# A delta-rule attention and SwiGLU kernel on one core: the order of work at its begin is rearranged

## The chip, the cores and the metric

The kernel runs on one NeuronCore of a Trainium2 chip. The core has five engines with an instruction queue each: TensorE (PE, matrix products), VectorE (DVE), ScalarE (ACT), GpSimd (POOL) and SyncE (SP, which here only issues DMAs). Each runs its own instructions strictly in the order of the program and waits for the others through semaphores. The metric is the device time of one execution in microseconds (us); times before are given as the median of three runs. A profile is the record of one execution, taken by the hardware profiler.

## The reference

Two blocks, one after the other. The first is a delta-rule attention over B = 4 batches, H = 8 heads, S = 768 steps, head dimension D = 48:

```python
k_n = k / (norm(k) + 1e-06)
for t in range(S):
    y[t]  = q[t] @ state
    v_old = state.T @ k_n[t]
    state = state + beta[t] * outer(k_n[t], v[t] - v_old)
```

The second is a SwiGLU feed-forward network on its output, laid out as 3072 tokens of 384 channels: `(silu(x @ w_gate) * (x @ w_val)) @ w_out`, with w_gate and w_val 384 x 1536 and w_out 1536 x 384. All data is float32.

## The kernel before

**Chunks.** The recurrence is cut into 12 chunks of 64 steps. Within a chunk it becomes matrix products: with K the turned (transposed) keys, K K^T is formed (`gram`, L501), a triangular system with it is inverted, the chunk's corrected values uu follow, and from them the chunk's output y, whose transpose is the input x of the network, and the new state. `turned` (L485) transposes k or q on PE; `gram_steps` (L501) forms K K^T or K Q^T into PSUM, and ACT copies it out (L526 for keys, L521 for queries). p_sb[c], the masked K Q^T, is needed only for y: its upper part is cleared by `under_mask` (L540), on GpSimd for chunk 0.

**Chunks 0 and 1.** They share one substitution on DVE (`first_substitution`, L712 and L718, 15 steps) over blocks of 16 steps. The blocks are put together by a short series: N = L Z (`n_products`, L745), where L are the scaled lower parts of K K^T (`low_copies`, L679) and Z the blocks' inverses (`spread_z`, L735 and L737, puts them into ztp[0]). `n_copies` (L751) takes N out of PSUM, and makes of half of it a copy whose two halves of partitions are exchanged (`n_back`, L755). Then uu comes from four groups of products (L959 for chunk 0 in `first_advance`; L1173 and L1200 for chunk 1 in `advance`): Z r, N times that, N again, N again, with DVE sums (`plus`, L1638) and ACT copies in between. The third group uses n_back. Then y = P uu with P = p_sb (L959 again), its transposes (L1048) and the copies to x (L1049), and the new state (`of_state`, L929; copied by L1054).

**The network.** `gate_val` (L1566) makes 256 columns of the hidden layer for one of the chunks 0 and 1: 12 products of PE in four quarters of three, then silu on ACT (L1575) and the product with the value half on DVE (L1577). From chunk 2 on a faster scheme with fewer products is used (L1411 and L1685). For the first two pieces of chunk 0, `chain` is called behind each quarter and puts one step of chunk 1's series there, with some conversion of weights.

**Weights.** They arrive in 42 pieces. `stage(n, after)` loads piece n on SP (L262); with `after` it first puts a one-element copy on GpSimd (L261) that reads piece `after`, so that piece n is only asked for once that one has landed. Each piece lands in a place that is free just then (`place_of`): tiles of h, of w_out, of ztp[1] ("z1"), and for the last ones the chunk 0 key tile ("zb", a_sb) and p_sb. `power_step` (two ACT instructions, L274 and L280) and `convert` (three DVE instructions, L293, L301, L313) turn a piece into the form that the products read. Converting a piece frees its place and issues the load that waits for it.

**Unread products.** `unread`, `small_unread` and `between` (L638, L648, L643) are products on PE whose results nobody reads.

**Order.** The order of all instructions is written out by hand (`tc.manual_schedule`): on each engine they run in the order in which the Python code emits them.

## Time and profile before

| what | us |
|---|---|
| median of 3 runs (lowest, highest) | 676.53 (675.25, 678.05) |
| the profiled execution | 671.1 |
| its span, first to last instruction | 669.4 |
| PE busy, share of the span | 649.4 (97%) |
| DVE busy | 477.2 (71%) |
| ACT busy | 280.4 (42%) |
| POOL busy | 199.4 (30%) |
| first product of the network (L1566) starts | 43.36 |

Times inside the profile are from the span's start. A line of the timeline has the start, the duration, the engine, the source line, the operation, what it writes and reads with the shape, how many were merged, and in brackets how long the engine was idle before it and what released it. A wait is put down to the event that came last. Matrix products of float32 appear as two records each in most rows; the transposes (L485, L1048) as one. The granted clock was 0.999 of full speed over the whole run.

### The profile page before, as it was taken

Reading aid. Unit: us, or ns where it says so; the run is one execution under the profiler, and the core shown is the slowest. Engines: PE = TensorE matmul, PEld = TensorE weight load, DVE = VectorE, ACT = ScalarE, POOL = GpSimd, SP = SyncE. Lnnn points to the kernel's source line nnn. Section 1 sums busy time; section 2 is a strip of 40 time slices with the busy share of each in tenths; the row PEclk is TensorE's granted clock in tenths of the full one; section 3 lists DMA queues with packets and bytes.
Section 4 is the critical chain, followed back from the end, with each engine's and each line's share of the span. In section 5 each row is a group of like instructions: output and inputs, shape, how many; then the busy total and the mean of one; then the engine's idle time right before and its main releaser. Section 6 shows DMA issues by size and latency. Waiting matters only on the chain.

```text
span 669.4 us, 25015 instructions
## 1 busy us (share of the span) xinstructions
PE 649.4 (97%) x10890; PEld 596.9 (89%) x10890; DVE 477.2 (71%) x992; ACT 280.4 (42%) x625; POOL 199.4 (30%) x310
## 2 busy tenths in 40 slices
PE   8889999999999999999999999989999989999997
PEld 5567887766899999999999999989999989999997
DVE  6779889998868767758667758667758655655562
ACT  4788846224335433434433433532433432433330
POOL 7121031035981032880031880030881000000000
PEclk9999999999999999999999999999999999999999
DMA  9666781005831451473453372434363432232321
GB/s 135 144 177 227 206 225 61 2 13 94 228 68 49 100 117 50 93 144 99 106 127 82 85 158 70 100 86 104 67 138 85 101 84 81 56 89 73 78 74 24
DMA packets 147439, 68.57 MB, mean 102 GB/s; under 512 B 123457, under 2 KB 126561, under 8 KB 147329
## 3 DMA queue, kind: packets, MB, share of 16 engines
q1 hardware_dynamic: 144992, 66.48, 41.5%
q8 instruction: 85, 1.39, 0.9%
q10 hardware_dynamic: 2080, 0.39, 0.4%
q14 instruction: 26, 0.20, 0.1%
q0 software_dynamic: 256, 0.10, 0.1%
HBM read 59.08 MB, written 7.86 MB: 100 GB/s over the span
## 4 chain that ended last, share of the span: by engine, by line
PE 81%; DVE 6%; DMA 4%; ACT 3%; issue 3%; SPq 2%; DVEq 0%; ACTq 0%
PE ffn L1411 38%; PE ffn L1685 20%; PE ffn L1595 4%; PE ffn L1566 4%; PE p_py L501 2%; SPq L172 1%; PE p_px L1173 1%; PE p_px L929 1%; PE p_px L501 1%; PE p_py L1075 1%; PE p_py L1092 1%; PE p_px L1156 1%; DMA h_f<-w_s 1%; DMA last_k<-in_k_dram 1%; DMA kn<-in_k_dram 1%
## 5 line engine op out<-in xcount | busy, mean ns | idle before, releaser
L1411 PE MATMUL ffn<-x_t,w_gv 128*128 128x128 f32 x800 | 108.8, 279 | 0.8 <-DVE p_sb L1635 0.6
L1411 PEld LDWEIGHTS ffn<-x_t,w_gv 128*128 128x128 f32 x800 | 97.4, 192 | 3.8 <-DVE p_sb L1635 1.2
L1445 ACT ACTIVATE sil<-ffn 128x256 f32<-128x256 f32 x100 | 36.5, 383 | 116.2 <-PE ffn L1411 109.6
L1411 PE MATMUL ffn<-x_ffn,w_gv 128*128 128x128 f32 x640 | 84.5, 275 | 0.0
L1685 PE MATMUL ffn<-wo_sb,h_f 128*128 128x192 f32 x480 | 83.9, 328 | 0.0
L1685 PEld LDWEIGHTS ffn<-wo_sb,h_f 128*128 128x128 f32 x480 | 77.9, 190 | 0.6
L1411 PEld LDWEIGHTS ffn<-x_ffn,w_gv 128*128 128x128 f32 x640 | 78.0, 192 | 0.3
L828 POOL TENSOR_TENSOR n_b<-mb,half 128x32 f32<-128x32 f32 x5 | 27.6, 5521 | 168.9 <-DVE mb L555 168.9
L586 POOL TENSOR_TENSOR h_f<-zb,mb 128x31 f32<-128x31 f32 (+15 forms) x124 | 69.0, 556 | 18.2 <-DVE mb L575 8.8
L592 POOL TENSOR_TENSOR zb<-zb,h_f 128x31 f32<-128x31 f32 (+15 forms) x124 | 71.2, 574 | 9.7
L1411 PE MATMUL ffn<-x_t,h_f 128*128 128x128 f32 x472 | 64.8, 280 | 1.3 <-DMA h_f<-w_s 1.0
L1411 PEld LDWEIGHTS ffn<-x_t,h_f 128*128 128x128 f32 x472 | 57.3, 192 | 3.3 <-DVE h_f L1635 0.8
L1446 DVE TENSOR_TENSOR h_f<-sil,ffn 128x256 f32<-128x256 f32 x100 | 39.4, 418 | 23.5 <-ACT sil L1445 23.4
L1107 ACT COPY x_ffn<-p_py 32x256 f32<-32x256 f32 (+3 forms) x108 | 39.4, 365 | 29.6 <-PE p_py L1092 27.9
L1635 DVE TENSOR_TENSOR ffn<-p_sb,ffn 128x512 f32<-128x512 f32 x40 | 27.8, 696 | 27.1 <-PE ffn L1411 26.4
L1638 DVE TENSOR_TENSOR ffn<-ffn,p_sb 128x512 f32<-128x512 f32 x40 | 27.2, 689 | 16.0 <-PE ffn L1411 16.0
L1685 PE MATMUL ffn<-last_k,h_f 128*128 128x192 f32 x200 | 36.0, 327 | 0.0
L1638 DVE TENSOR_TENSOR o_sb<-o_sb,ffn 128x192 f32<-128x192 f32 x50 | 17.5, 350 | 24.4 <-PE ffn L1685 23.8
L1566 PE MATMUL ffn<-x_t,w_gv 128*128 128x256 f32 x144 | 33.4, 384 | 0.0
L1685 PEld LDWEIGHTS ffn<-last_k,h_f 128*128 128x128 f32 x200 | 32.9, 190 | 0.1
L1566 PE MATMUL ffn<-x_ffn,w_gv 128*128 128x256 f32 x144 | 31.9, 380 | 0.0
L1411 PE MATMUL ffn<-x_ffn,h_f 128*128 128x128 f32 x232 | 30.9, 276 | 0.0
(345 smaller groups left out, 1176.3 us busy)
## 6 DMA issues: line engine op xcount, KB each, us to landing
h_f<-w_s SPq DMA_DIRECT2D x81, 256.0 KB, 2.8
more_w<-w_s SPq DMA_DIRECT2D x27, 256.0 KB, 2.6
vin<-in_v_dram SPq DMA_DIRECT2D x48, 96.0 KB, 3.3
out_dram<-o_sb SPq DMA_DIRECT2D x48, 96.0 KB, 2.2
kn<-in_k_dram SPq DMA_DIRECT2D x20, 192.0 KB, 4.4
zt<-in_moe_w_out_dram SPq DMA_DIRECT2D x6, 384.0 KB, 4.9
qpad<-in_q_dram SPq DMA_DIRECT2D x36, 64.0 KB, 3.0
w_s<-h_f SPq DMA_DIRECT2D x7, 256.0 KB, 4.3
```

The lines of the kernel that those rows point to most:

```text
L586: engine.tensor_tensor(out=t_v, in0=zb[:, 0 : j + 1, j : j + 1].to_broadcast([128, j + 1, m]), in1=mb[:, j : j + 1, j + 1 : R].to_broadcas ...
L592: engine.tensor_tensor(out=zb[:, 0 : j + 1, j + 1 : R], in0=zb[:, 0 : j + 1, j + 1 : R], in1=t_v, op=ALU.add,)
L828: nc.gpsimd.tensor_tensor(out=n, in0=mb.rearrange("p j i -> p (j i)")[:, 0 : R * R : R + 1], in1=half, op=ALU.pow,)
L1107: nc.scalar.copy(x_all[at % 128 : at % 128 + rows, at // 128].rearrange("p (bp b i) -> p bp b i", bp=NB, b=2), p[64 * half + lo : 64 * hal ...
L1411: nc.tensor.matmul(p[:, u], w(u), moving, start=start and u == 0, stop=True, skip_group_check=True,)
L1445: nc.scalar.activation(silu_of, p[:, 0:2], ACTF.Silu)
L1446: nc.vector.tensor_tensor(out=h_of(c, PAIRS[r][e % 3], e // 3), in0=silu_of, in1=p[:, 2:4], op=ALU.mult)
L1566: nc.tensor.matmul(ps[name][:, i], w_sb[:, t, (f + i) * 128 : (f + i + 1) * 128], xts[c][:, t], start=(t == 0 and i == 0), stop=(t == KT - 1),
L1595: nc.tensor.matmul(p_o, hs[c, f - f % 2][:, f % 2, bp * 128 : (bp + 1) * 128], wo_sb[:, f], start=(f == 0), stop=(f == FT - 1),)
L1635: nc.vector.tensor_tensor(out=out, in0=a, in1=b, op=ALU.subtract)
L1638: nc.vector.tensor_tensor(out=out, in0=a, in1=b, op=ALU.add)
L1685: nc.tensor.matmul(p[x, part], a(f - f % 2)[:, f % 2], b(f), start=not begun and f == 0, stop=f == FH - 1, skip_group_check=True,)
```

## The change

The changed kernel computes the same. All edits lie in the begin and in the handing over to the network's first pieces. (Line numbers of the changed kernel are lower by up to 14: its product L950 is L959 here, its L1552 is L1566.)

- The unread products: 16 small ones become two large ones, four further places are gone or moved, four stand where two stood before n_products, and the four of `between` are removed from `first_advance`.
- K K^T of chunk 2 is formed right behind its turning, in the pair of banks px, before chunk 3 is turned. `low_copies` of chunks 0 and 1 come ahead on ACT, right behind the copies of q's turning.
- n_back is copied on GpSimd from the copy of N in SBUF (new L744), where DVE (chunk 0) and ACT (chunk 1) copied it from PSUM.
- The masks of chunk 0's p_sb (two L540 on GpSimd) are emitted behind the first step of `first_advance` and behind the stagings of pieces 8 and 9. They stood behind the stagings of pieces 6 and 7, one each. Stagings 8 and up follow that first step, too. So GpSimd's order from there is: one-element copies for pieces 2 to 7, the two copies of n_back, copies for 8 and 9, the two masks, copies for 10 to 13, two `spread_z` of chunk 1, copies for 14 to 17, and later the two copies of chunk 1's n_back.
- `spread_z` of chunk 1 moves from DVE and ACT to GpSimd (L726).
- The state of chunk 0 (`of_state` and its copy) is made behind the first quarter of the first gate_val.
- `chain` runs over the first three gate_vals (12 quarters, in 8 of which a step of chunk 0 or 1 stands), with fewer pieces converted in each.
- The last pieces land in ztp[0] ("z0", two places), p_sb and z1; the key tile a_sb is used no more for that.

```diff
@@ -230,13 +230,13 @@
         places[n] = words(hp[n])
     place_of = [(n, 0) for n in range(10)] + [("wo", 8 * H_), ("z1", 0)]
     in_wo, in_z1 = [("wo", 2 * H_ * n) for n in range(4)], [("z1", 2 * H_), ("z1", 0)]
-    in_work = [("zb", 0), ("p_sb", 0)]
+    in_z0 = [("z0", 0), ("z0", 2 * H_)]
     place_of += [("wo", H_ * n) for n in range(8)]
     place_of += [("z1", H_ * n) for n in (2, 3, 1, 0)]
-    place_of += in_wo + in_work + (in_z1 + in_work) * 3
+    place_of += in_wo + in_z0 + (in_z1 + [("p_sb", 0)] + in_z0) * 2 + in_z1
 
     beta_s = places["wo"].bitcast(FP32)[:, 6 * H_ : 6 * H_ + S]
-    LATE = {"zb": 18, "p_sb": 12}
+    LATE = {"z0": 18, "p_sb": 12}
     freed_by = {}
     for n, (name, lo) in enumerate(place_of):
         m = 2 * pieces[n][4]
@@ -612,7 +612,6 @@
             l_sb[c] = a[:, R * R * c : R * R * (c + 1)].rearrange(
                 "p (h k) -> p h k", k=C
             )
-        places["zb"] = words(a)[:, 0 : 2 * PIECE]
         first_of["flat"] = new_mb().rearrange("p k i -> p (k i)")
         first_of["diag"] = first_of["flat"].rearrange("p (j h) -> p h j", j=R)
         first_of["zb"] = places["z1"].bitcast(FP32)[:, 4 * H_ - 1056 : 4 * H_]
@@ -636,16 +635,6 @@
 
         for _ in range(count):
             nc.tensor.matmul(p[0:R], half, half[:, 0:1].to_broadcast([128, 512]))
-
-    def between(columns):
-        p = banks("p_t", 0)[0]
-        of = half[:, 0:1].to_broadcast([128, columns])
-        nc.tensor.matmul(p[0:R, 0:columns], half, of)
-
-    def small_unread(count, p):
-
-        for _ in range(count):
-            nc.tensor.matmul(p[0:C, 0:C], ident[0:C, 0:C], ident[0:C, 0:C])
 
     def first_gram(c, tag):
 
@@ -752,7 +741,9 @@
                 n_sb[c][:, par].rearrange("p bp j i -> p (bp j i)"), p_n[par]
             )
         for x in range(2):
-            back(n_back[c][half_of(x)], p_n[1][half_of(1 - x)])
+            back(n_back[c][half_of(x)], n_sb[c][half_of(1 - x), 1].rearrange(
+                "p bp j i -> p (bp j i)"
+            ))
 
     n_back = {}
 
@@ -948,10 +939,10 @@
     def first_advance():
 
         zt = ztp[0][:, 0].rearrange("p (par bp j) i -> p par bp j i", par=2, bp=NB)
-        r, pq = vin.pop(0), p_sb.pop(0)
+        r = vin.pop(0)
         p_n = banks("p_n", 2)
         n_products(0, p_n)
-        n_copies(0, p_n, (nc.scalar.copy, nc.vector.tensor_copy), nc.vector.tensor_copy)
+        n_copies(0, p_n, (nc.scalar.copy, nc.vector.tensor_copy), nc.gpsimd.tensor_copy)
 
         def product(p, at, flip, weights, moving):
             for j in range(NJ):
@@ -992,7 +983,6 @@
                 lambda par, b, j: v[there(par, b), 1 - par, bp, j],
             )
             nc.scalar.copy(uu[:, :, bp], pairs[bp])
-        between(128)
         yield MORE
         for bp in range(NB):
             product(
@@ -1007,7 +997,6 @@
             plus(t[:, 0:2, bp], v[:, :, bp], pairs[bp])
             for x in range(2):
                 nc.scalar.copy(t[half_of(x), 2, bp], t[half_of(1 - x), 0, bp])
-        between(128)
         yield MORE
         for bp in range(NB):
             product(
@@ -1018,10 +1007,9 @@
                 lambda par, b, j: t[there(par, b), 1 - par, bp, j],
             )
             plus(uu[:, :, bp], t[:, 1:3, bp], pairs[bp])
-        between(256)
-        spread_z(1, 0, nc.vector)
         held_loads[26] = lambda: load_v(2)
         yield
+        pq = p_sb.pop(0)
         y = work.tile([128, NB, NJ, 2, D], FP32, name="y", tag="r", bufs=2)
         for bp, copy in enumerate((nc.scalar.copy, nc.vector.tensor_copy)):
             product(
@@ -1047,10 +1035,8 @@
                 at = slice(k * 128, (k + 1) * 128)
                 nc.tensor.transpose(p_f[bp][:, k], y_f[:, bp, at], ident)
             copy(x_v[:, :, bp], p_f[bp])
-            if bp == 0:
-                between(256)
+        yield
         p_s = of_state(0, uu)
-        spread_z(1, 1, nc.scalar)
         nc.scalar.copy(state, p_s)
         yield
 
@@ -1948,29 +1934,27 @@
         first_diag(1, p_g[1])
         spread_beta(copy_a)
         turned(0, True, 0)
+        low_copies(0, p_g[0])
+        low_copies(1, p_g[1])
         nc.vector.transpose(first_of["mb"][:, 0 : R * R], first_of["flat"])
         r_b = first_n()
         first_scale(r_b)
         for n in range(6):
             stage(n, n - 2 if n > 1 else None)
         load_v(1)
-        small_unread(16, banks("p_t", "py")[0])
+        unread(2, banks("p_t", "py")[0])
         turned(2, False, "py")
         first_q = [gram_steps(0, True, 0, (copy_a, copy_a))]
         next(first_q[0])
-        low_copies(0, p_g[0])
-        unread(1, banks("p_t", "py")[0])
+        gram(2, False, "px", (copy_a, copy_a))
         turned(3, False, "py")
-        unread(1, banks("p_t", "px")[0])
+        unread(1, banks("p_t", 2)[0])
         turned(1, True, "px")
-        gram(2, False, "py", (copy_a, copy_a))
-        unread(1, banks("p_t", "px")[0])
-        low_copies(1, p_g[1])
         gram(3, False, "py", (copy_a, copy_a))
         first_q.append(gram_steps(1, True, "px", (copy_a, copy_a)))
         next(first_q[1])
         next(first_q[0])
-        unread(2, banks("p_t", 2)[0])
+        unread(4, banks("p_t", 2)[0])
         first_substitution()
         first_z()
         some, others = slice(0, 1), slice(1, NB)
@@ -1981,20 +1965,22 @@
         scale_v(0)
         next(first_q[1])
         stage(6, 4)
-        next(first_q[0])
         stage(7, 5)
-        next(first_q[0])
-        for n in range(8, 10):
-            stage(n, n - 2)
-        for n in range(10, 18):
-            stage(n, n - 3)
-        for n in range(18, 23):
-            stage(n)
         zb_1 = work.tile([128, R, R], FP32, name="zb", bufs=1)
         new_nt(0, spare_of_q, state_flat[:, LEAD : LEAD + 512])
         new_nt(1, zb_1.rearrange("p k i -> p (k i)"), spare_of_q[:, 0:512])
         gens["advance", (0,)] = [first_advance(), 0]
         step("advance", advance, 0)
+        for n in (8, 9):
+            stage(n, n - 2)
+        next(first_q[0])
+        next(first_q[0])
+        for n in range(10, 14):
+            stage(n, n - 3)
+        for x in range(2):
+            spread_z(1, x, nc.gpsimd)
+        for n in range(14, 23):
+            stage(n, n - 3 if n < 18 else None)
         power_step(0)
         step("advance", advance, 0)
         converts_first(0)
@@ -2006,7 +1992,6 @@
         step("advance", advance, 0)
         power_step(1)
         step("advance", advance, 0)
-        step("advance", advance, 0)
         converts_first(4)
         for n in (3, 5):
             power_step(n)
@@ -2015,25 +2000,31 @@
         power_step(6)
 
         went = []
+        chain_at = (0, 1, 3, 4, 6, 7, 9, 10)
 
         def chain(_):
 
-            if not went:
-                p_n = banks("p_n", 2)
-                n_products(1, p_n)
-                n_copies(1, p_n, (copy_a, copy_a), copy_a)
-            step("advance", advance, 1)
-            n, ahead = ((1, 7), (2, 6), (4, 4))[len(went)] if len(went) < 3 else (2, 4)
-            went.append(n)
-            if len(went) in (4, 5):
-                next(first_q[1])
-            convert(todo[:n], ahead)
-            del todo[:n]
+            at = len(went)
+            went.append(1)
+            n, ahead = (1, 2, 4, 1, 2, 1, 2, 1, 2, 1, 2, 1)[at], (7, 6, 4, 4)[min(at, 3)]
+            if n:
+                convert(todo[:n], ahead)
+                del todo[:n]
+            if at in chain_at:
+                if at in chain_at[4:6]:
+                    next(first_q[1])
+                if at == 0:
+                    step("advance", advance, 0)
+                    p_n = banks("p_n", 2)
+                    n_products(1, p_n)
+                    n_copies(1, p_n, (copy_a, copy_a), nc.gpsimd.tensor_copy)
+                else:
+                    step("advance", advance, 1)
 
         pairs = [(c, f) for c in range(2) for f in range(0, 8, 2)]
         pairs += [(c, f) for f in range(8, FT, 2) for c in range(2)]
         for at, (c, f) in enumerate(pairs):
-            early = c == 0 and f < 4
+            early = c == 0 and f < 6
             if c == 1 and f == 0:
                 finish(1)
                 second_inverse.append(invert(1))
```

## Prediction

> **What bounds the kernel now.** I read the page first, then the span cut into stretches of 5 us, then the timelines of PE, GpSimd and SP in the begin.
>
> ```profile
> PE 649.4 (97%) x10890; PEld 596.9 (89%) x10890; DVE 477.2 (71%) x992; ACT 280.4 (42%) x625; POOL 199.4 (30%) x310
> ...
> PE 81%; DVE 6%; DMA 4%; ACT 3%; issue 3%; SPq 2%; DVEq 0%; ACTq 0%
> ```
>
> PE is busy for 97% of the span and is 81% of the chain that ended last. So what the begin costs is the time until PE has network products to do, and what it waits for afterwards.
>
> ```profile
> 25.00:30.00 5.00, 3.60 (x107) 1.92 (x102) 4.01 (x9) 4.21 (x10) 0.56 (x3) 1.00 0.43 128
> 30.00:35.00 5.00, 4.33 (x232) 3.67 (x224) 3.33 (x6) 3.54 (x9) 1.60 (x3) 1.00 0.49 132
> 35.00:40.00 5.00, 3.40 (x132) 2.51 (x135) 3.98 (x9) 2.58 (x9) 1.42 (x2) 1.00 0.66 167
> ...
> 65.00:70.00 5.00, 5.00 (x26) 4.43 (x25) 5.00 (x17) 3.93 (x11) 0.00 (x0) 1.00 0.73 223
> ...
> 110.00:115.00 5.00, 3.39 (x21) 2.76 (x20) 4.58 (x11) 4.21 (x10) 0.00 (x0) 1.00 0.00 0
> ```
>
> The columns are the stretch, its length, busy us of PE, PE's weight loads, DVE, ACT and POOL, then clock, DMA share and GB/s. From 65 us PE is full, but DVE is, too; it converts weights. At 110 PE loses 1.61 us.
>
> ```profile
> 1.03 4.90 PE L638 MATMUL p_px<-half 128*32 128x512 f32 x6 [1.03 <-DVE half L322]
> ...
> 27.92 1.91 PE L638 MATMUL ffn<-half 128*32 128x512 f32 x4
> 29.76 1.16 PE L745 MATMUL ffn<-zt,a_sb 64*64 64x64 f32 x64
> ...
> 38.84 0.68 PE L959 MATMUL p_px<-uu,p_sb 64*64 64x48 f32 x32 [0.73 <-DVE uu L1638]
> ...
> 42.28 1.15 PE L929 MATMUL p_px<-uu,kn 64*64 64x48 f32 x64
> 43.36 1.56 PE L1566 MATMUL ffn<-x_t,w_gv 128*128 128x256 f32 x6
> ```
>
> Chunk 0's series runs from n_products at 29.76 over the product with p_sb at 38.84 to the first network product at 43.36. GpSimd in that time:
>
> ```profile
> 32.63 0.18 POOL L261 COPY h_f<-h_f 128x1 uint32<-128x1 uint32 x1 [0.45 <-DMA h_f<-in_moe_w_gate_dram]
> 32.77 1.28 POOL L540 TENSOR_TENSOR p_sb<-p_sb,mask_q 128x512 f32<-128x512 f32 x1
> 35.75 0.19 POOL L261 COPY h_f<-h_f 128x1 uint32<-128x1 uint32 x1 [1.70 <-DMA h_f<-in_moe_w_val_dram]
> 35.89 1.28 POOL L540 TENSOR_TENSOR p_sb<-p_sb,mask_q 128x512 f32<-128x512 f32 x1
> 40.27 0.18 POOL L261 COPY h_f<-h_f 128x1 uint32<-128x1 uint32 x1 [3.11 <-DMA h_f<-in_moe_w_gate_dram]
> 40.90 0.18 POOL L261 COPY h_f<-h_f 128x1 uint32<-128x1 uint32 x1 [0.45 <-DMA h_f<-in_moe_w_val_dram]
> ```
>
> These one-element copies are those for pieces 6, 7, 8 and 9; each waits until pieces 4, 5, 6 and 7 have landed. The two masks stand between them, at 32.77 and 35.89, ahead of the waits that end at 40.27 and 40.90. The loads behind those late waits are on SP:
>
> ```profile
> 32.59 3.25 SPq L185 DMA_DIRECT2D vin<-in_v_dram  x4
> 35.94 0.57 SPq L262 DMA_DIRECT2D h_f<-in_moe_w_gate_dram  x1
> 36.60 0.38 SPq L262 DMA_DIRECT2D h_f<-in_moe_w_val_dram  x1
> ```
>
> Piece 6 can't be asked for before 35.94: SP first issues four loads of v, and those stand behind piece 5, which was released at 32.00. Nothing in the change moves this part of SP's or GpSimd's queue.
>
> **Part 1: fewer unread products, K K^T of chunk 2 ahead, low copies ahead.** Removed are 16 small products (2.07 us, 13.55), three of 1.05 us (17.81, 19.81, 23.10), two before n_products (1.91) and four short ones (0.41, 0.41, 0.62, 0.62): 9.2 us. Added are seven large ones at 0.92 to 1.05: 6.7 us. ACT sits idle for 2.39 us before 16.68; the twelve low copies (two rows of 1.68 us) now start at 14.29 and end at 17.65, so the copies of chunk 2's turned keys start 1.0 us later and K K^T of chunk 2 on PE at about 18.3. Following each copy and product from there by the rows, the last K Q^T ends near 24.7 and the four unread products end near 28.3. Z is ready at 28.31 as before, because DVE's substitution is untouched. So n_products starts at 28.4 rather than 29.76: a gain of 1.35 us. It disappears in part 2. Two pauses of PE with no releaser (1.40 at 26.03, 0.74 at 34.80) may move or vanish; they have cover there, too.
>
> **Part 2: n_back on GpSimd.** The two copies come behind the one-element copy for piece 7, which ends at 35.94; N itself is in SBUF at about 30.3. GpSimd has no row for 64x512 copies. The nearest are a memset of 128x256 (0.31, so 0.6 for twice the length) and the two-operand mask (1.28). I take 0.75, nearer the memset since a copy reads one operand; ends: 0.5 and 1.28 each. N_back is ready at 37.4 (36.9 to 38.5). The third group of chunk 0 (34.01 before) waits for it. From 34.01 to the last sum of uu at 39.16 were 5.15 us, 0.74 of them a pause; so uu is there at 41.8 (41.3 to 43).
>
> **Part 3: the masks.** They stand behind the copies for pieces 8 and 9, which end at 41.08, and take 2 x 1.28: ready at 43.64. That is later than uu for either price of part 2, so it decides. Both masks are needed by the second product of the group that starts at 38.84 now; it starts at 43.69, **4.85 us later**. Then its two groups (0.68 and 0.66, without the 0.34 pause of before), DVE's copies of y (0.36 and 0.72), the transposes (0.55) and the copy to x (0.56), with 0.05 between: 47.4 for the first network product, against 43.36. That is **+4.05**. DVE's third conversion (piece 4, done at 44.06 now) follows the copy to x and is done at 48.5, just when the third product wants it: +0.1, cover gone.
>
> **Part 4: the state behind the first quarter.** Its 1.09 us of PE lay ahead of 43.36 and now lie behind: **+1.09**. The ACT copy of it comes behind seven pieces' conversions (0.67 each) and is done at 52.1; the product that needs it (L1156 now) comes at 52.7. No wait.
>
> **Part 5: spread_z of chunk 1 on GpSimd.** DVE loses 0.65 and ACT 1.19. GpSimd does it behind the copy for piece 13, near 47.2, at 0.5 (memset) to 1.9 (the mask, half as much again for the turned read) each; at 1.28 it ends at 49.8, and n_products of chunk 1 wants it at 50.1. At the upper end PE would wait 1 us there. Pieces 14 and up are asked for about 1.5 us later, under a shift of 4.
>
> **Part 6: chunk 1's series over three gate_vals.** Now PE waits 0.56 at 52.49 (for an ACT copy) and 0.72 at 61.23 (for DVE). With two quarters between some steps I find both copies ready: **-1.28**, with 0 as the other end. Pieces 12 to 17 are converted by 68.4, before the third gate_val's value half needs the last, at 71.9.
>
> **Part 7: last pieces in Z's tile.** The 1.61 at 113.56 is PE waiting for ACT's copy of K K^T of chunk 4, which stands behind piece 41's power step, which waits until 109.67 for its load, which waits for DVE. Silu products of DVE run 4 to 5 us behind PE there (104.00 for a piece that PE ended near 99.3). DVE's conversions begin 4.5 us later than before (piece 4) and DVE has few waits to give back, so I keep the 1.61: **0**, ends -1.6 and +0.5. The free key tile does not help: the copy is queued behind piece 41 all the same.
>
> **Sum:** 4.05 + 0.1 + 1.09 - 1.28 + 0 = **+4.0 us**. The profiled execution would go from 671.1 (span 669.4) to 675.1. The median is 5.4 above the profiled one; I carry the difference over: 676.5 + 4.0 = 680.5.
>
> **Rivals.** *PE goes cold.* In the new begin PE has nothing from about 32.0 until n_back at 37.4, then little until 43.7. The rows show PE at two speeds with the granted clock at 1.00 in both: three unread products took 4.90 us at the start, two took 1.91 at 27.92, so 1.63 against 0.96 each. The longest idle stretch of before behind the start is 1.6 us, so its trace doesn't show that a pause brings the slow speed back. If it does, the p_sb groups cost 1.3 more, the transposes on the path 0.5, and a stretch like the 4.9 us of the start does 2.45 us less of work: +4.2, against which the 1.61 is given back: 676.5 + 4.0 + 4.2 - 1.6 = 683.1. [...]
>
> *The shift is taken up later (no change).* If PE's lateness lets DVE and ACT catch up, the 1.61 goes: 4.0 - 1.6 = 2.4, so 678.9. For it: DVE has waits of 1.87 and 1.02 between 80 and 95. Against it: these are behind ACT, which shifts with PE.
>
> *The masks come in time (faster).* If pieces 6 and 7 landed by 36.1 instead of 40.9, the masks would be done by 38.8 and parts 1, 4, 6 and 7 would be left: -1.35 + 1.09 - 1.28 - 1.61 = -3.15, 673.4. Against it are the SP rows: piece 6 is only asked for at 35.94, and the two masks alone take 2.56.
>
> **Chances.** Forecast 0.42, cold 0.30, taken up 0.16, faster 0.12. The range from 676.0 to 685.0 reaches from part 6 and 7's better ends nearly together to the cold case with spread_z's wait. What a measurement of this kernel can tell from no change is 0.5%, 3.4 us: the forecast with its own spread of 1.5 us is slower by that in two thirds of its cases, the cold case nearly always. So faster 0.12, same 0.28, slower 0.60.
>
> **What would show it.** In the profile after: GpSimd's masks back to back at about 41.1 and ending at 43.6, behind one-element copies released by DMA; n_back's copies at 36; PE idle before the third and fifth group; the first network product at 47.4. Cold shows as L1566's rows of three products at over 2 us instead of 1.56. Part 6 shows as no waits over 0.3 between 50 and 75, part 7 as a pause of about 1.6 near 117. The prediction is wrong if the pieces land earlier, or if PE's wait at 113 is gone.

## The result and the profile after

The changed kernel takes **671.98 us** (median of 9 runs, 668.29 to 673.54); the kernel before takes 675.25 us (9 runs in the same set, 670.27 to 678.05). The ratio is 0.9936, with a 95% interval of 0.9907 to 0.9965: faster by 0.64%, where the prediction had 680.5 and slower. The profiled execution of the changed kernel took 672.2 us with a span of 670.5. That is its median, while the profiled execution of before (671.1) lay 4.2 us under the median of this set. Profile against profile the kernel became 1.1 us *slower*, median against median 3.3 us faster; both have to be explained.

The page of the kernel after: the busy time of TensorE (PE), the granted clock in 40 slices of the span, and the shares of the chain that ended last.

```profile
PE 651.4 (97%) x10854; PEld 598.6 (89%) x10854; DVE 476.7 (71%) x989; ACT 279.1 (42%) x622; POOL 208.0 (31%) x316
...
PEclk9968999999999999999999999999999999999999
...
PE 83%; DVE 6%; DMA 4%; SPq 3%; ACT 2%; issue 2%; POOL 0%; DVEq 0%; ACTq 0%; POOLq 0%
```

PE has 36 matmul records fewer (18 unread products), and "issue", the time with no releaser in the profile, is 2% of the chain instead of 3%. In the third and fourth slice (34 to 67 us) the clock digit falls to 6 and 8. GpSimd in the begin (the timeline of the kernel after: start, duration, engine, line, instruction, and in brackets the idle time before it):

```profile
36.65 0.18 POOL L261 COPY h_f<-h_f 128x1 uint32<-128x1 uint32 x1 [0.50 <-DMA h_f<-in_moe_w_val_dram]
36.90 1.26 POOL L744 COPY state<-qpad 64x512 f32<-64x512 f32 x2
...
40.76 0.33 POOL L261 COPY h_f<-h_f 128x1 uint32<-128x1 uint32 x1 [0.34 <-DMA h_f<-in_moe_w_val_dram]
41.05 2.67 POOL L540 TENSOR_TENSOR p_sb<-p_sb,mask_q 128x512 f32<-128x512 f32 x2
...
47.06 4.09 POOL L726 TENSOR_SCALAR zt<-mb,m_rows 128x512 f32<-128x512 f32 x2
```

The copies of N stand behind piece 7's one-element copy, and the masks behind that of piece 9; they end at 43.7. The two spread_z take 2.05 us each. PE in the same stretch:

```profile
27.96 1.16 PE L734 MATMUL ffn<-zt,a_sb 64*64 64x64 f32 x64
...
38.21 0.34 PE L950 MATMUL p_px<-uu,state 64*64 64x48 f32 x1 [4.44 <-POOL state L744]
...
44.61 0.68 PE L950 MATMUL p_px<-uu,p_sb 64*64 64x48 f32 x32 [2.61 <-DVE uu L1624]
...
46.37 1.76 PE L1036 MATMUL ffn<-ident,y 128*128 128x128 f32 x6 [0.36 <-ACT y L1024]
48.88 3.41 PE L1552 MATMUL ffn<-x_t,w_gv 128*128 128x256 f32 x6 [0.74 <-ACT w_gv L274]
```

N_back comes 4.4 us too late for the third group, the masked product starts at 44.61, and the first network product at 48.88 instead of 43.36. Its first three products (six records) take 3.41 us instead of 1.56. The stretches of the kernel after (the columns are those of the prediction's second fence; the clock is the third from the end) show why:

```profile
30.00:35.00 5.00, 2.10 (x89) 1.60 (x81) 1.14 (x3) 3.11 (x8) 0.37 (x2) 1.00 0.48 141
35.00:40.00 5.00, 1.79 (x62) 1.79 (x62) 0.56 (x1) 0.00 (x0) 1.59 (x4) 0.51 0.80 206
...
45.00:50.00 5.00, 3.90 (x61) 2.83 (x53) 2.86 (x6) 4.40 (x14) 3.15 (x4) 0.53 0.66 213
50.00:55.00 5.00, 4.86 (x109) 3.48 (x111) 4.83 (x13) 3.20 (x9) 2.48 (x5) 0.50 0.41 121
...
110.00:115.00 5.00, 5.00 (x143) 4.29 (x141) 4.86 (x12) 3.36 (x7) 0.00 (x0) 1.00 0.65 203
```

PE ran at half clock from 35.1 to 41.9 and from 45.3 to 55.6 us. At 110 to 115 us it is full: the 1.61 us wait of before has gone. So the begin became slower, about as forecast, and yet the kernel is faster. The rest of the document is about where the time came back.

### The profile page after: what moved, and what is told of

Its sections match the earlier page's. It is cut to its first block, busy times and chain, and to the rows that moved or that the text cites. A ratio compares the mean times of both kernels' runs of the same rounds, so it can differ in the third digit from the quotient of the medians.

```text
span 670.5 us, 24923 instructions
## 1 busy us (share of the span) xinstructions
PE 651.4 (97%) x10854; PEld 598.6 (89%) x10854; DVE 476.7 (71%) x989; ACT 279.1 (42%) x622; POOL 208.0 (31%) x316
## 3 DMA queue, kind: packets, MB, share of 16 engines
q8 instruction: 85, 1.39, 0.9%
## 4 chain that ended last, share of the span: by engine, by line
PE 83%; DVE 6%; DMA 4%; SPq 3%; ACT 2%; issue 2%; POOL 0%; DVEq 0%; ACTq 0%; POOLq 0%
PE ffn L1397 39%; PE ffn L1671 20%; PE ffn L1581 4%; PE ffn L1552 4%; DMA h_f<-in_moe_w_val_dram 2%; PE p_px L1159 2%; PE p_px L920 2%; SPq L139 1%; PE p_py L1061 1%; PE p_px L1142 1%; PE p_py L501 1%; PE p_py L1078 1%; PE p_px L501 1%; SPq L185 1%; PE p_py L902 1%
## 5 line engine op out<-in xcount | busy, mean ns | idle before, releaser
L1397 PEld LDWEIGHTS ffn<-x_t,w_gv 128*128 128x128 f32 x800 | 97.4, 192 | 3.6 <-DVE p_sb L1621 1.3
L819 POOL TENSOR_TENSOR n_b<-mb,half 128x32 f32<-128x32 f32 x5 | 30.4, 6073 | 161.1 <-DVE mb L555 161.1
L586 POOL TENSOR_TENSOR h_f<-zb,mb 128x31 f32<-128x31 f32 (+15 forms) x124 | 70.7, 570 | 19.2 <-DVE mb L575 9.7
L1552 PE MATMUL ffn<-x_t,w_gv 128*128 128x256 f32 x144 | 35.4, 397 | 0.9 <-ACT w_gv L274 0.7
L1552 PEld LDWEIGHTS ffn<-x_t,w_gv 128*128 128x128 f32 x144 | 27.2, 195 | 5.7 <-ACT w_gv L274 1.1
L1552 PE MATMUL ffn<-x_ffn,w_gv 128*128 128x256 f32 x144 | 31.9, 380 | 0.0
```

The lines of the kernel that those rows point to most:

```text
L586: engine.tensor_tensor(out=t_v, in0=zb[:, 0 : j + 1, j : j + 1].to_broadcast([128, j + 1, m]), in1=mb[:, j : j + 1, j + 1 : R].to_broadcas ...
L819: nc.gpsimd.tensor_tensor(out=n, in0=mb.rearrange("p j i -> p (j i)")[:, 0 : R * R : R + 1], in1=half, op=ALU.pow,)
L1397: nc.tensor.matmul(p[:, u], w(u), moving, start=start and u == 0, stop=True, skip_group_check=True,)
L1552: nc.tensor.matmul(ps[name][:, i], w_sb[:, t, (f + i) * 128 : (f + i + 1) * 128], xts[c][:, t], start=(t == 0 and i == 0), stop=(t == KT - 1),
```

## The experiments

Each row has the median of all executions of that kernel and its ratio to the kernel before, run in turn on the same chip. The ratio compares runs taken in turn, so it is not the quotient of two medians. The rows come from sets on several chips; the median of before was 675.99 beside the first four rows, 676.28 beside the next four and 678.35 beside the three after them.

| run | edit | us | ratio (95% interval) |
|---|---|---|---|
| before_again | none | 677.19 | 1.0023 (0.9990 to 1.0057) |
| masks_first | after; masks and N's copies ahead of pieces 6 to 9 | 670.43 | 0.9928 (0.9904 to 0.9952) |
| masks_late | before; masks behind pieces 8, 9 | 683.90 | 1.0124 (1.0090 to 1.0158) |
| fewer_unread | before; 18 unread products fewer | 673.04 | 0.9961 (0.9932 to 0.9991) |
| after_padded | after; 18 unread products more | 676.66 | 1.0004 (0.9975 to 1.0033) |
| spread_back | after; spread_z of chunk 1 on DVE | 670.97 | 0.9933 (0.9905 to 0.9960) |
| masks_and_spread | masks_first and spread_back | 668.07 | 0.9874 (0.9833 to 0.9915) |
| masks_spread_warm | masks_and_spread; five unread products more | 668.13 | 0.9877 (0.9831 to 0.9922) |
| before_shifted | before; 16 unread products fewer, same PE time | 672.44 | 0.9941 (0.9906 to 0.9976) |
| before_wide | before; four unread products made wider | 674.95 | 0.9980 (0.9946 to 1.0013) |
| masks_spread_wide | masks_spread_warm, stream as in after | 668.52 | 0.9884 (0.9842 to 0.9926) |
| before_third | none, one profile | 677.83 | one execution |

**The begin, undone and done alone.** masks_late moves the masks in the kernel before and nothing else:

```diff
         stage(6, 4)
-        next(first_q[0])
         stage(7, 5)
-        next(first_q[0])
         for n in range(8, 10):
             stage(n, n - 2)
+        next(first_q[0])
+        next(first_q[0])
```

> The kernel before with only the two masks moved behind the copies for pieces 8 and 9, as the change has them. Theory that the late masks cost what the prediction gave them: the product with p_sb starts near 43.7 instead of 38.84, and the kernel is slower by 4 to 5 us than before, by 6 to 8 with a stretch at half clock. Rival (taken up later): within 2 us of before.

It was slower by 1.2%, about 8 us. PE's longest waits in masks_late (us in total, times, longest):

```profile
PE p_px L959 <- POOL p_sb L540: 5.2, 2, 4.4
PE ffn L1411 <- issue: 3.0, 3, 1.9
PE p_py L911 <- issue: 2.5, 1, 2.5
PE p_px L485 <- ACT a_sb L529: 2.3, 1, 2.3
```

The wait on the masks is the forecast's 4.85 to within half a microsecond. The other three lines are already in the profile of before, at 1.8, 2.0 and 1.6 us; here their totals are larger, and half-clock windows stand at 43.3 to 50.1, behind the stall at L485 (121.8 to 125.2) and behind L911's pause (555.3 to 558.7). So part 3's mechanism costs what was forecast, or more.

masks_first goes the other way, in the kernel after:

```diff
-        stage(6, 4)
-        stage(7, 5)
...
-        for n in (8, 9):
-            stage(n, n - 2)
         next(first_q[0])
         next(first_q[0])
+        for n in (6, 7, 8, 9):
+            stage(n, n - 2)
```

> The changed kernel with n_back's copies and both masks put ahead of the copies for pieces 6 to 9 on GpSimd (behind that for piece 5). Theory that GpSimd's queue delays the begin by 5 us and cools PE: n_back is copied at about 33 instead of 36.9, the masks end near 37 instead of 43.7, the first network product comes at 42 to 43.5 instead of 48.9, and the clock falls to half in no stretch or in one window of 3.4 us; 6 us below the changed kernel, so 664 to 667. Rival (the begin's lateness is taken up later by the conversions of DVE and ACT): the first network product is early, and the end moves by less than 2 us: 670 to 672.

The first network product came at 42.0 instead of 48.9, but the gain was gone 10 us later: 670.43 lies in the range of the expected rival, not of the theory. The clock wasn't kept either; there were four windows of half clock in three stretches (32.2 to 35.6, 42.4 to 45.8, 49.3 to 56.1) where one at most was expected. PE's longest wait in masks_first, and GpSimd's timeline at that place:

```profile
PE ffn L734 <- POOL zt L726: 5.5, 1, 5.5
```

```profile
46.93 0.29 POOL L261 COPY wo_sb<-wo_sb 128x1 uint32<-128x1 uint32 x1 [2.37 <-DMA wo_sb<-in_moe_w_gate_dram]
47.20 4.41 POOL L726 TENSOR_SCALAR zt<-mb,m_rows 128x512 f32<-128x512 f32 x2
```

Chunk 1's spread_z on GpSimd stands behind piece 13's copy, at 47.2 whatever PE does, and takes 4.4 us. In the kernel after, PE is so late that it doesn't notice; with an early begin it is the next wait. Two runs separate this. spread_back puts both on DVE in the kernel after, masks_and_spread does the same in masks_first:

```diff
             plus(uu[:, :, bp], t[:, 1:3, bp], pairs[bp])
+        spread_z(1, 0, nc.vector)
...
             copy(x_v[:, :, bp], p_f[bp])
+        spread_z(1, 1, nc.vector)
         yield
...
-        for x in range(2):
-            spread_z(1, x, nc.gpsimd)
```

> The kernel after with chunk 1's two spread_z on VectorE (0.65 us each in the kernel before), one behind the last sum of chunk 0's series, one behind the last copy of x, instead of GpSimd (2.05 us each). Theory (in the kernel after no TensorE wait hangs on them, since the third group of products is late anyway): 671 to 673, within 0.5% of the kernel after. Rival (GpSimd's two spreads hold up the copies that issue pieces 14 to 17 behind them, and so the conversions): 1 to 2 us faster, 669 to 671.

> The kernel with the masks ahead of the copies for pieces 6 to 9 (masks_first), and chunk 1's two spread_z on VectorE as in spread_back. Theory (the whole shift of the begin was GpSimd's order: masks at 4 to 5 us, then the spreads that took the 5.5 us back): first network product at 42 us as in masks_first, no wait of TensorE on zt at 52 us, every later mark about 5 us earlier than in the kernel after (151 to 153 instead of 158.2 for chunk 1's first product with the state), time 664 to 667. Rival (a clock or conversion bound takes it back: half clock or waits on the weights between 45 and 75 us): the marks within 2 us of the kernel after and a time of 669 to 672.

spread_back can't be told from the kernel after (670.97 against 671.98, ratios 0.9933 and 0.9936); its time lies at the edge between the two expected ranges. masks_and_spread, at 668.07, is 1.26% under before and the fastest here together with its two variants. PE's timeline in masks_and_spread:

```profile
34.63 0.25 PE L950 MATMUL p_px<-uu,state 64*64 64x48 f32 x1 [0.48 <-POOL state L744]
...
38.84 1.11 PE L950 MATMUL p_px<-uu,p_sb 64*64 64x48 f32 x32
...
43.68 2.90 PE L1554 MATMUL ffn<-x_t,w_gv 128*128 128x256 f32 x6 [0.74 <-DVE x_t L1038]
48.25 1.43 PE L734 MATMUL ffn<-zt,a_sb 64*64 64x64 f32 x64
```

The masked product waits for nothing, and chunk 1's n_products start 5.7 us earlier than in the kernel after (53.96 there). Chunk 2's first product of q with the state (L1144 in before) comes at 152.4, within the 151 to 153 expected; the expectations call it chunk 1's first product with the state, and from here on it is called chunk 2's mark. The time was 1 us above the 664 to 667 expected.

**Where the late gain comes from.** The kernel before has two PE pauses without a releaser that no part of the prediction counted: 1.8 us at 444 (L1411) and 2.0 us at 543 (L911). In the kernel after there is none over 0.3 us behind 60 us. PE's timeline in before at the two places, and then that of the kernel after at the second:

```profile
441.65 0.61 PE L1411 MATMUL ffn<-x_ffn,more_w 128*128 128x128 f32 x4
444.08 0.60 PE L1411 MATMUL ffn<-x_ffn,more_w 128*128 128x128 f32 x4 [1.82 <-issue]
...
539.79 1.22 PE L911 MATMUL p_py<-t,z 32*32 32x32 f32 x120
543.00 0.26 PE L911 MATMUL p_py<-t,z 32*32 32x32 f32 x8 [1.99 <-issue]
```

```profile
543.04 1.29 PE L902 MATMUL p_py<-t,z 32*32 32x32 f32 x128
```

One theory: they belong to a place in PE's instruction stream, and 18 products fewer ahead of them moved that place onto other work. The rival: they depend on when data or work arrives. The first run is the kernel before unchanged, the second takes away its unread products alone:

> The kernel before, unchanged, profiled a second time. Theory P (pauses): PE's pauses that no engine releases (1.82 at 444 us and 1.99 at 543 us in the profile before, none in the profile after) belong to the place in PE's instruction stream, so they return here at the same instructions, and the typical execution is longer than the first profile's 671.1 us by more of them. Theory B (begin): the first profile caught a lucky begin, with the granted clock at 0.999; a typical one has a stretch at half clock in the first 60 us, a mean clock of 0.98 to 0.99, and is then near 675. Theory N: both kernels are equal, and the ratio of 0.9936 is chance; then this run's median comes out within 0.3% of the other runs of before, which it must in any case.

```diff
-        between(128)
...
-        between(128)
...
-        between(256)
...
-            if bp == 0:
-                between(256)
...
-        small_unread(16, banks("p_t", "py")[0])
+        unread(2, banks("p_t", "py")[0])
```

> The kernel before with two large unread products for the 16 small ones and without the four of between: 18 products fewer, as in the changed kernel, and nothing else of the change. Theory P: every later instruction of PE stands where it stands in the changed kernel, so the pauses at 444 and 543 us vanish or shrink and the kernel gains 2 to 4 us. Theory B: the begin is as before or cools (fewer products that keep PE busy), and the kernel is equal or slower by up to 3 us.

In before_again the pauses came back at the same two instructions (1.7 and 1.4 us). fewer_unread lost about 6 us in the begin (half clock from 36.9 to 47.1; chunk 2's mark at 157.2 instead of 151.3), had neither pause, and was still 0.4% faster than before. Both theories allow that, since its begin had moved. after_padded settles it: the kernel after, with as many products more as it has fewer, in a place where PE waits anyway.

```diff
-        unread(4, banks("p_t", 2)[0])
+        small_unread(22, banks("p_t", 2)[0])
```

> The kernel after with 22 products of 32x32 where it has 4 unread ones of 128x32 ahead of n_products of chunk 0: 18 more products, so that from there on TensorE's instructions stand at the same places of its stream as in the kernel before. Place theory (the pauses of 1.8 us at 444 us and 2.0 us at 543 us in the kernel before, which have no releaser, hang on where a run of short products falls in TensorE's stream): pauses of 1.4 to 2 us come back near 450 us (L1411) and 549 us (L911 of before, L902 or so of after), and the time rises by 3 to 4 us over the kernel after, to 675 to 676. Rival (these pauses hang on the data transfers or on when the work arrives, which the other parts of the change moved): no pause over 0.7 us after 260 us and a time within 1 us of the kernel after, 671 to 673.

It took 676.66, and the whole gain was gone (ratio 1.0004). PE's timeline in after_padded has only two waits over 0.3 us between 410 us and the end:

```profile
448.63 0.49 PE L1402 MATMUL ffn<-x_ffn,more_w 128*128 128x128 f32 x3 [1.49 <-issue]
...
548.14 0.26 PE L907 MATMUL p_py<-t,z 32*32 32x32 f32 x7 [2.37 <-issue]
```

(L1402 and L907 here are L1411 and L911 in before.) They stand behind 7731 and 9383 matmul records, in before behind 7730 and 9382, with every other part of the change in place. So the place theory holds. The other profiles bear it out: all six with 10890 matmul records have both pauses (1.4 to 2.5 us) at these places, though PE gets to the first one anywhere between 444 and 455 us, and of the eight with fewer records only masks_spread_warm has a pause of over 0.4 us at either. before_shifted is the counterpart: the kernel before, with the begin's PE time kept and its stream 32 records shorter.

```diff
-        between(128)
+        between(384)
...
-        between(128)
+        between(384)
...
-        between(256)
...
-            if bp == 0:
-                between(256)
...
-        small_unread(16, banks("p_t", "py")[0])
+        unread(2, banks("p_t", "py")[0])
```

> The kernel before with 16 unread products fewer at about the same time on TensorE: two of 512 columns (2.1 us) for the 16 of 32x32 (2.1 us), and the four between the groups of chunk 0's series (768 columns in all) as two of 384. All that follows stands 32 matmul records earlier in TensorE's stream. Place theory: the profile's pauses without a releaser at 444 us (1.8 us) and 543 us (2.0 us) shrink to 1 us or less in all while the begin keeps its marks (chunk 1's first product with the state at 151 to 153 us), so 2.5 to 3.5 us faster than the kernel before at equal clock, a median of 672 to 674. Rival (the pauses hang on something else that fewer_unread moved by its 6 us of delay): both pauses stay, 675 to 677.

Both pauses were gone, and its ratio of 0.9941 (a median of 672.44) is as much of a gain as the whole change brought. Its profiled execution is not a clean one: a stall of 2.9 us at L485 and a wait of 2.2 us for a load at 352 us, each with 3.4 us of half clock behind it; chunk 2's mark was at 153.7, a little outside the 151 to 153 expected. The verdict rests on the median and on the missing pauses.

**Why the typical execution of before is slower than its profile.** Two profiles of before (671.1 and 671.7 us) had a granted clock of 1.00 from 5 us to PE's last product, but among 61 executions of it in the first two sets of experiments (the two longest left out), the 23 with a mean clock of 0.9955 or more have a median of 673.75, the other 38 one of 677.16. By estimate (3.41 x 0.5 / 670) a window of 3.41 us at half clock takes 0.0025 off the mean clock of a run of 670 us, so this parts executions with one such window at most from those with two or more. Two runs looked for the place.

```diff
-        between(128)
+        between(512)
...
-        between(256)
+        between(512)
```

> The kernel before with its four unread products between the groups of chunk 0's series 512 columns wide each instead of 128, 128, 256 and 256: no instruction more or fewer, 1.3 us more of TensorE's time, in gaps where it waits 0.3 to 0.7 us. Clock theory (most executions of the kernel before lose 3 to 4 us to one or two windows of half clock in the begin, its profiled executions did not): the mean granted clock is 0.997 or more in most executions, and the median 673 to 674.5, the pauses at 444 and 543 us staying. Rival (the slower executions of before have another cause, or the wider products only delay the groups): clocks of 0.992 to 0.995 as before and a median of 676 to 677.5.

before_wide is inconclusive: 9 of its 12 executions had a mean clock of 0.995 or more, against 6 of the 22 of before beside it, but only 5 had the 0.997 that was expected of most, its interval reaches 1.0013, and its profiled execution was itself one of the long ones (677.39). It did show two windows of half clock: one in the begin, from 28.8 to 32.2, and one from 117.6 to 121.0, behind 2.9 us of stall at L485. So one more profile of before was taken:

> The kernel before, unchanged, one more profile. Where the typical execution of before loses the 3 to 4 us that its two profiled ones did not lose: stall theory (ScalarE's copies of chunk pair 1's first gram products stand behind the conversion of pieces of the output weights that come late, so TensorE stands at L485 near 114 us for over 2.2 us, and a window of half clock follows, as in the profiles of before_wide, before_shifted and masks_late): if this execution is over 674 us, that stall is 2.3 to 3 us with 3.41 us of half clock behind it. Begin theory (the loss lies in half-clock windows ahead of 60 us): half clock there instead, and the stall at 114 us is 1.6 to 2.3 us without one. If the execution is under 673 us, neither is told apart, and the clock is 1.00 until the end.

This execution took 677.83 us, close to the median. PE's waits, and two stretches with a clock under 1:

```profile
PE p_py L911 <- issue: 2.5, 1, 2.5
PE p_py L959 <- issue: 2.4, 3, 1.0
PE ffn L1411 <- issue: 2.1, 2, 1.6
PE p_px L485 <- ACT a_sb L529: 2.0, 1, 2.0
```

```profile
115.00:120.00 5.00, 5.00 (x20) 4.40 (x21) 4.20 (x15) 1.61 (x3) 0.00 (x0) 0.66 0.01 2
```

```profile
545.00:550.00 5.00, 2.47 (x82) 2.31 (x69) 0.83 (x2) 1.02 (x2) 0.00 (x0) 0.87 0.20 74
550.00:555.00 5.00, 5.00 (x37) 5.00 (x37) 2.39 (x4) 1.89 (x4) 0.00 (x0) 0.78 0.29 67
```

Half clock stands at 115.3 to 118.7, behind the stall at L485, and at 548.7 to 552.2, behind L911's pause; none stands ahead of 60 us. For this execution the begin theory is out; before_wide's window at 28.8 leaves it open for others. The stall theory is right on the place, though at 1.95 us this stall is shorter than the 2.3 to 3 expected (before_again had one of 2.28 and no half clock, so its length alone doesn't decide), and it named only half of the loss: the second window hangs on the late pause.

**The clock in the begin.** masks_spread_warm adds five unread products between the groups (the expectation counts six, and five for before, which has four). masks_spread_wide takes two wide ones instead, leaves out one at two earlier places, and has the stream of the kernel after.

```diff
             nc.scalar.copy(v[:, :, bp], pairs[bp])
+        between(256)
         yield MORE
...
             nc.scalar.copy(uu[:, :, bp], pairs[bp])
+        between(128)
         yield MORE
...
+        between(128)
...
+        between(256)
...
+            if bp == 0:
+                between(256)
```

```diff
-        between(256)
...
-        between(128)
+        between(512)
...
-        between(128)
+        between(512)
...
-        between(256)
...
-            if bp == 0:
-                between(256)
...
-        unread(2, banks("p_t", "py")[0])
+        unread(1, banks("p_t", "py")[0])
...
-        unread(4, banks("p_t", 2)[0])
+        unread(3, banks("p_t", 2)[0])
```

> masks_and_spread with six unread products (three of 256 columns, two of 128, and one more of 256 behind the first group) between the groups of chunk 0's series, where the kernel before has five. Theory (the half clock comes from TensorE's gaps between the groups, and filling them keeps it at 1.0): no half-clock window between 30 and 60 us and 1 to 3 us faster than masks_and_spread. Rival (the gaps are too long for six short products, or the half clock lies under waits anyway): within 1 us of masks_and_spread, half clock still there.

> masks_spread_warm with two unread products of 512 columns instead of its five between the groups, and one fewer at two earlier places, so that TensorE's stream stands as in the kernel after (masks_spread_warm has five products more, and a pause of 1.3 us at 542 us). Place theory: no pause over 0.5 us near 542 us, and 666.5 to 667.5. Rival (the pause is a matter of chance, or the half clock of the begin comes back): 668 to 669.

masks_and_spread had half clock from 35.3 to 48.9, masks_spread_warm only from 44.0 to 47.4, yet the first network product came at 43.7 and 44.0, chunk 2's mark at 152.4 in both, and the times are equal (668.07 and 668.13). So the longer half clock cost nothing by that mark; what covered it is not shown. masks_spread_wide had no pause near 542, as the place theory expected (masks_spread_warm had 1.3 us there), but its 668.52 lies in the rival's range, and the gain could not be told from nothing. Its profile has what masks_spread_warm's lacks: a stall of 2.46 us at L485, and two windows of half clock ahead of 60 us (32.6 to 36.1 and 42.9 to 46.3).

## Why the prediction was wrong

The table gives the start of the same work in five profiles, counted in matmul records back from the last one (the first row is the first network product).

| place | before | before_third | after | after_padded | masks_and_spread |
|---|---|---|---|---|---|
| first network product | 43.4 | 43.9 | 48.9 | 47.9 | 43.7 |
| 8526 from the end (chunk 2's mark) | 151.3 | 154.4 | 158.2 | 156.0 | 152.4 |
| 7100 | 227.4 | 231.6 | 233.6 | 231.3 | 227.9 |
| 3165 (ahead of L1411's pause) | 441.5 | 446.2 | 446.9 | 446.3 | 442.6 |
| 3150 (behind it) | 445.2 | 449.6 | 448.5 | 449.6 | 444.3 |
| 1512 (ahead of L911's pause) | 540.8 | 545.3 | 544.0 | 545.5 | 539.8 |
| 1500 (behind it) | 543.2 | 548.3 | 544.3 | 548.3 | 540.0 |
| 690 | 592.8 | 599.5 | 593.8 | 597.9 | 589.6 |
| last | 665.0 | 671.7 | 666.1 | 670.1 | 661.8 |

Against the typical execution of before (column before_third), the kernel after loses 5.0 us by its first network product. It is 3.8 behind at chunk 2's mark and 0.7 at 3165, gains 1.8 over L1411's pause and 2.7 over L911's, and 1.6 more over the work behind that, where before_third is at half clock: 5.6 us ahead at the end. Of the 3.1 us between chunk 2's mark and 3165, 2.3 are PE waits: those of over 0.3 us there sum to 3.65 in before_third and to 1.31 in after. Why they are shorter, the runs don't show.

before_third itself is 3.1 us behind the first profile at chunk 2's mark, 4.7 at 3165 and 6.7 at the end; its two half-clock windows stand ahead of that mark and behind row 1512, and the rest of the 6.7 isn't explained.

- **Part 1:** right. n_products at 27.96 (forecast 28.4), and the gain vanished in part 2.
- **Part 2:** right in place, N_back at 38.2 (37.4; the upper end was 38.5). Each copy took 0.63 (0.75).
- **Part 3:** right in place and nearly in size, wrong in what decides. Masks from 41.05 to 43.72 (41.1 to 43.6), the masked product at 44.61 (43.69), the first network product at 48.88. The prediction had the masks come last, but the wait at 44.61 ends with uu: N_back was 0.8 later, and the groups behind it ran at half clock. The 1.5 us over 47.4 are these 0.9 and the transposes, 1.76 for the six instead of 1.10 in before.
- **Part 4:** not refuted. The kernel after is 5.5 late at the first network product and 7.0 at chunk 2's mark, against the first profile; 1.09 of the difference was forecast.
- **Part 5:** right that it costs nothing here, for the wrong reason. 2.05 us each is above the upper end of 1.9, and PE's lateness hid it; with an early begin it costs PE 5.5 us of waiting (masks_first).
- **Part 6:** right. No wait of 0.3 us or more stands between 52 and 118 us.
- **Part 7:** wrong, 0 was taken. The 1.61 us wait went (its end was -1.6); in before_third a half-clock window stands behind this wait, and the profile of the kernel after has none there. Which part of the change took the wait away is not shown. Of the seven profiles of kernels built on after, six have 0.8 us of it or less, but masks_spread_wide has 2.46; the seven built on before have 1.6 to 2.9.
- **The sum and its base:** this is the step that failed. The sum ends with part 7 at 113 us and holds everything behind it for unchanged. The two pauses of 1.8 and 2.0 us, listed as PE's longest waits in the profile before, were left out, because the prediction looked for what the edit touches and not for what it shifts. That is a missing term of -4.2 us by the columns before and after (2.1 at each pause, counting from the row ahead to the row behind). Then "the median is 5.4 above the profiled one; I carry the difference over" took as constant what belongs to the kernel before: the half clock behind L485's stall and L911's pause. The profile of the kernel after has neither, and it lies at its median. Against the first profile the sum closes like this: 4.0 forecast, -1.6 (part 7), 4.6 more by chunk 2's mark (what is left of the 7.0 there; the half clock, and N_back's 0.8), -1.6 from the mark to 3165 (not explained) and -4.2 at the pauses make +1.2, where the profiled executions differ by 1.1. That the 4.6 and the pauses nearly cancel is chance.
- **The rival "PE goes cold"** happened: PE had nothing from 33.8 to 38.2, and half clock is on record from 35.1, 1.3 us into that. It did not decide the sign. The stretches at half clock in the traces up to PE's last product are multiples of 3.41 us (3.41 in before_third, 6.83 and 10.24 in the kernel after, 13.65 in masks_and_spread); the idle directly ahead of them was 1.3 us at 35.1 in the kernel after, and 1.95 and 2.5 in before_third. The rival's estimated price of 4.2 us reckons with half the speed over a stretch of 4.9 us, a term that no run shows: the rows of before make 1.63 against 0.96 us a product. What the runs showed in its place is a granted clock of 0.50 for 17.1 us in all in the begin of the kernel after; its price was not measured by itself, the 4.6 above hold it. In masks_and_spread, against masks_spread_warm, 10.24 us more of half clock cost nothing by chunk 2's mark. The first profile has its granted clock on record only from 5.4 us, so the prediction's unread products at 1.03 us don't show two speeds at one clock.
- **The rival "masks come in time"** had the right direction for the wrong reason: the masks came at 43.7.
- **The rival "taken up later"** had the 1.61 go, which it did, but a late begin alone isn't why: masks_late and fewer_unread, 7.4 and 3.9 us late at the first network product, keep 2.3 us of that wait, and masks_and_spread, 0.3 us late, has none.

## What to carry to other kernels

A wait that no instruction releases can belong to a position in an engine's instruction stream: 18 products more ahead of the two places brought 1.49 and 2.37 us of waiting back (after_padded), 16 fewer took 1.8 and 2.0 away (before_shifted). So where an edit changes the number of instructions ahead of such waits, list them over the whole span and count them as terms that may go or come. When the profiled execution lies well off the median, find out from the clock of the other executions what they have that the profile lacks before carrying the difference over: it belongs to that kernel, not to the change. And what is moved to a queue that waits for loads arrives when the loads do, so its cost shows only once the rest has become early enough: spread_z, behind piece 13's copy at about 47 us in both kernels, cost no wait in the kernel after and 5.5 us in masks_first.

## What the runs showed of the hardware

- **Pauses at fixed places of the stream.** The profiles of before, before_again, before_third, after_padded, masks_late and before_wide have 1.4 to 2.5 us behind 9382 or 9383 matmul records and 1.5 to 1.9 us behind 7730 or 7731; masks_spread_warm has 1.3 us behind 9382, where other work (L1410) stands. The later one stands behind 120 of a run of 128 short products (L911), which takes 1.1 us from first to last where nothing interrupts it; the earlier one in before begins at 442.3, 1.5 us behind the end of such a run. The page's queue list has 85 packets under "instruction" in queue 8, 1.39 MB, so 16 KB each. In all 13 pauses the next product starts 1.1 to 1.5 us behind the end of such a packet; of all products behind 60 us only 3 to 7% do, by run. The ties to the place and to the packets are shown; what the packets hold, and whether a late one is the cause, is not shown.
- **Half clock without a long idle.** In before_third a stall of 1.95 us (L485) and a pause of 2.5 us (L911) were each followed by 3.41 us of half clock, where the prediction had 5.4 us without work (32.0 to 37.4) in mind. Stalls of 2.28 us in before_again, 2.32 in fewer_unread and 2.46 in masks_spread_wide were not, nor was L911's 2.5 in before_wide, so the length alone doesn't decide. The window behind L911's pause cost about 1.6 us by the end of before_third.
- **GpSimd.** A 64x512 copy took 0.63 us in the kernel after, a 128x512 product with one operand and a turned read 2.05 us there and 2.2 in masks_first, against 1.28 for the plain two-operand mask in before (1.34 in the kernel after).
